# A spectral filter's channel products split by parity of the frequency, with 64-row tails in both row halves, and the skip weights added on GpSimd

## The chip, the cores and the metric

The kernel runs on one core of one Trainium2 chip. The metric is the device time of one execution in microseconds (us); smaller is better. All data are 32-bit floats.

A core has five engines that this text calls as the profile does. PE is TensorE, which multiplies matrices out of SBUF into the banks of PSUM; PEld are its loads of the stationary operand. DVE is VectorE, ACT is ScalarE, POOL is GpSimd, and SP is the engine whose queue issues most DMAs. Each engine works through its own instructions in the order in which the program lists them, and waits for the others by semaphores.

## What is computed

The input x has 2048 rows and 640 channels. The output mixes two branches with a gate for each row: a state-space branch (a long convolution along the rows, its kernel made from 128 modes for each channel, with a skip term) and a branch that filters x in a two-dimensional Fourier domain (rows and channels).

```python
def _A_ref(u, log_A_real, A_imag, C_real, C_imag, log_dt, D_skip):
    ...
    P = jnp.exp((A * dt[:, None])[:, :, None] * pos[None, None, :])
    K = 2.0 * jnp.einsum("dn,dnl->dl", C, P).real
    ...
    Kf = jnp.fft.rfft(K, L2)
    Uf = jnp.fft.rfft(u_t, L2)
    y = jnp.fft.irfft(Uf * Kf[None, :, :], L2)[:, :, :L]
    ...
    return y + u * D_skip[None, None, :]

def _B_ref(x, w_r, w_i):
    X = jnp.fft.rfft2(x, axes=(-2, -1))
    W = w_r + 1j * w_i
    y = jnp.fft.irfft2(X * W, s=(S, D), axes=(-2, -1))
    return y

g = sigmoid((x * gate_w).sum(-1, keepdims=True))
return g * a + (1 - g) * b
```

## The kernel before

Every Fourier transform is a product with a table of sines and cosines on PE. The length of 4096 along the rows is taken apart in two stages (`stage1`, `stage2`); the transform along the 640 channels, which only the filter has, is done by four tables of 160 or 161 columns in the forward direction and by two tables of 321 columns backward.

The program is five phases. Phase P makes the parameters of the convolution kernel. Phase A (its first half, up to line 442) transforms x along the rows and stores the result in device memory (`u_d`). Its second half, the filter (lines 445 to 599), runs 9 turns (eight of 128 rows of frequencies, one of 64). Phase B makes the convolution kernel in 40 steps of 16 channels (`mags`, `phases`, `trig`, `prods`, `kgen`; five steps share one group, since ACT changes its table between exponentials and sines). Phase C transforms the first quarter of that kernel along its length. Phase D multiplies the transforms, goes back and mixes with the gate; it begins when all the others have been issued.

The order of the work is written out by hand. Phases A and C form one stream of the program and phases P and B another; both are generators that yield a cost after each piece of PE work. `merge((194.0, ga), (76.8, gl))` in line 229 always continues the stream with the smaller sum of yielded costs divided by its weight. The two streams are first advanced without a cost up to a fixed point in phase A (`T.pin`, in the second of its four quarters). So the yields and the two weights decide which pieces stand beside which on each engine.

One turn of the filter has these parts, taken in an order that overlaps three turns. `front` (line 471) loads a turn's rows and its weights `ww`, and folds the 640 channels into sums and differences `fg`: DVE takes one half of them and GpSimd the other (lines 487, 488). `transposes` (line 492) brings `fg` to channels on partitions in three chunks, `CH`, of 128, 128 and 65 rows, and later `pm` back in three chunks, `CF`, of 107 rows. `channels` (line 511) makes four products, each in a bank of its own: for each of two parities one matmul over 128 rows and one over the 65 rows of the last chunk. ACT copies two of the four banks to `bc`; DVE adds and subtracts them with the other two (lines 526, 527). `filt` (line 529) multiplies by the weights on DVE. `back1` (line 545) goes back along the channels for 128 rows at a time (17 blocks in all): two products of three matmuls with 107 rows and 321 columns, one copied by ACT to `o`, and two DVE instructions that add or subtract the two halves into `qq`, the second with a reversed output. `back2` (line 560) makes the last product with `qq` and stores it. The three PSUM banks of pool `f_ps` serve all of these.

In phase B, `kgen` (line 685) makes the convolution kernel for 8 columns of channels in one bank. After every second step four small matmuls with the identity (line 703) add the skip weights `dsk` to the column of position 0; ACT then copies the bank to `kt` (line 704). After every tenth step SP stores `kt` to `k_d` (line 706); there is one buffer for `kt`. The store shares SP's queue with the filter's loads.

## Time and profile before

| | us |
|---|---|
| three runs | 604.54, 610.11, 607.86 |
| median of the runs | 607.86 |
| profiled execution, from its first to its last instruction (span) | 605.9 |
| L696, PE, phase B's products, busy | 63.0 |
| L639 and L650, PE, phase B's exponents and phases, busy | 58.9 and 43.3 |
| L681 and L683, GpSimd, phase B's products, busy | 55.4 and 55.5 |
| L703, PE, skip weights, busy (160 instructions) | 5.4 |
| mean granted clock of PE | 0.963 |

For the profiled execution the span is the time on record; it lies 1.96 us under the median of the runs and inside their spread.

In the profile a line like "L552 PE MATMUL p_eo<-td,pmt 107*128 107x321 f32 x204 | 67.5, 450 | ..." reads: line 552 of the kernel, engine, operation, the tile written and the tiles read, rows by columns of the stationary operand, rows by columns of the moving one, how many; then the time in which at least one of them ran, in us; the mean duration of one, in ns; and the idle time of the engine just before, with what ended it. Each 32-bit matmul of the program is two passes in the profile, so 102 matmuls show as 204. Instructions of one engine overlap a little at their ends, and those of PE a good deal, so count times mean is more than the busy time. A row of busy tenths divides the span into 40 slices of 15.1 us, one digit each; 9 is 90% or more.

### The profile page before, as it was taken

What the parts mean: (1) busy time and instruction counts of PE and PEld (TensorE: products, weight loads), DVE (VectorE), ACT (ScalarE), POOL (GpSimd) and SP (SyncE); (2) the same over time, 40 slices, a digit from 0 to 9 for tenths busy, and PEclk for the clock granted to TensorE, in tenths of its full rate; (3) what the DMA queues carried; (4) which work ended last, traced back from release to release, by engine and by line L of the source; (5) the groups of instructions that cost most, each with busy time, mean ns of one, the idle gap of its engine ahead of it and who ended that gap; (6) DMA issues with size and microseconds to landing.
All of it is one profiled execution on the core that took longest, in us unless ns stands there. A gap on an engine that the chain in (4) does not pass through costs nothing. (4 is left out here: it accounts for less than half of the span.)

```text
span 605.9 us, 16674 instructions
## 1 busy us (share of the span) xinstructions
PE 537.6 (89%) x7084; PEld 409.0 (68%) x7084; DVE 496.4 (82%) x748; ACT 364.5 (60%) x659; POOL 263.0 (43%) x246
## 2 busy tenths in 40 slices
PE   9598979988989989989889989898969999999875
PEld 7586647766766667666667676656859877787651
DVE  5971597598899998999998899879397696995965
ACT  4556775476857777899697897798712322232120
POOL 4931153054346344444515344416253447547533
PEclk9999999999979997999897999999998999999979
DMA  8777203235612321243250232006684989879767
GB/s 342 292 283 264 90 2 130 92 133 196 245 45 66 100 85 41 79 125 125 67 140 22 55 96 110 29 23 212 212 346 146 364 274 287 313 254 322 241 211 269
DMA packets 48082, 101.96 MB, mean 168 GB/s; under 512 B 3316, under 2 KB 32776, under 8 KB 46248
## 3 DMA queue, kind: packets, MB, share of 16 engines
q1 hardware_dynamic: 24888, 67.74, 32.1%
q10 hardware_dynamic: 20080, 22.52, 11.9%
q0 software_dynamic: 3040, 10.65, 5.3%
q8 instruction: 55, 0.90, 0.6%
q14 instruction: 19, 0.16, 0.1%
HBM read 60.91 MB, written 39.98 MB: 167 GB/s over the span
## 5 line engine op out<-in xcount | busy, mean ns | idle before, releaser
L349 PE MATMUL p_s<-t,w 128*64 128x160 f32 x1056 | 91.6, 311 | 11.2 <-ACT ut L383 6.0
L681 POOL TENSOR_TENSOR y<-e,sc 128x512 f32<-128x512 f32 x40 | 55.4, 1384 | 89.2 <-DVE x L676 46.7
L349 PEld LDWEIGHTS p_s<-t,w 128*64 128x64 f32 x1056 | 75.9, 137 | 22.3 <-ACT ut L383 6.6
L641 ACT ACTIVATE e<-p_e 128x512 f32<-128x512 f32 x120 | 68.6, 602 | 23.6 <-PE p_e L639 21.4
L683 POOL TENSOR_TENSOR y<-e,sc 128x512 f32<-128x512 f32 x40 | 55.5, 1388 | 44.9 <-ACT sc L667 32.0
L696 PE MATMUL p_k<-x,y 128*32 128x64 f32 x2560 | 63.0, 227 | 11.2 <-POOL y L681 6.1
L696 PEld LDWEIGHTS p_k<-x,y 128*32 128x32 f32 x2560 | 45.2, 112 | 39.6 <-issue 24.2
L552 PE MATMUL p_eo<-td,pmt 107*128 107x321 f32 x204 | 67.5, 450 | 3.9 <-ACT pmt L506 3.9
L337 ACT COPY t<-p_s 128x512 f32<-128x512 f32 x40 | 24.5, 621 | 69.0 <-PE p_s L336 45.5
L653 DVE SCALAR_TENSOR_TENSOR q<-q,p_p 128x512 f32<-128x512 f32 x80 | 53.4, 680 | 13.5 <-ACT q L652 13.3
L639 PE MATMUL p_e<-rm,par 128*128 128x512 f32 x120 | 58.9, 520 | 5.2 <-ACT e L641 3.7
L803 POOL TENSOR_TENSOR t<-ma 64x320 f32<-64x320 f32 x32 | 27.9, 873 | 64.2 <-DVE ma L798 54.8
L652 ACT ACTIVATE q<-p_p 128x512 f32<-128x512 f32 x80 | 46.4, 591 | 6.6 <-PE p_p L650 6.2
L552 PEld LDWEIGHTS p_eo<-td,pmt 107*128 107x128 f32 x204 | 37.7, 194 | 18.4 <-ACT pmt L506 6.4
L678 DVE TENSOR_TENSOR x<-e,cx 128x1024 f32<-128x1024 f32 x40 | 48.5, 1212 | 1.9 <-ACT cx L669 1.9
L817 PE MATMUL p_i<-t,w 128*64 128x160 f32 x528 | 45.1, 308 | 4.4 <-POOL t L804 3.4
L336 PE MATMUL p_s<-c,kt 128*64 128x128 f32 x640 | 44.3, 277 | 3.9 <-DVE mb L799 2.0
L336 PEld LDWEIGHTS p_s<-c,kt 128*64 128x64 f32 x640 | 39.5, 138 | 12.2 <-issue 6.9
L650 PE MATMUL p_p<-rp,par 128*128 128x512 f32 x80 | 43.3, 546 | 4.6 <-DVE q L653 4.5
L819 ACT COPY s<-p_i 128x640 f32<-128x640 f32 x32 | 21.8, 693 | 38.8 <-PE p_i L817 38.7
L817 PEld LDWEIGHTS p_i<-t,w 128*64 128x64 f32 x528 | 39.1, 141 | 8.9 <-POOL t L804 4.0
L798 DVE TENSOR_TENSOR ma<-p_s,us 128x640 f32<-128x640 f32 (+1 forms) x36 | 28.2, 784 | 20.3 <-PE p_s L349 13.3
(153 smaller groups left out, 1186.4 us busy)
## 6 DMA issues: line engine op xcount, KB each, us to landing
u_d<-ut SPq DMA_DIRECT2D x32, 320.0 KB, 3.2
us<-u_d ACTq DMA_DIRECT2D x16, 640.0 KB, 6.0
s_d<-s ACTq DMA_DIRECT2D x15, 640.0 KB, 6.7
t<-s_d SPq DMA_DIRECT2D x14, 640.0 KB, 5.7
ww<-in_w_l SPq DMA_DIRECT2D x8, 642.0 KB, 3.8
ue<-u_d SPq DMA_DIRECT2D x8, 640.0 KB, 4.1
k_d<-kt SPq DMA_DIRECT2D x4, 1280.0 KB, 8.7
kt<-k_d SPq DMA_DIRECT2D x8, 640.0 KB, 5.9
```

Of the source, the lines that this page charges most:

```text
L336: nc.tensor.matmul(p[64 * ri:64 * ri + 64, j, :], src(i + j), e1[ri], start=True, stop=True)
L349: ins = nc.tensor.matmul(p[64 * j:64 * j + 64, i, 160 * ri:160 * ri + 160], w2[:, x, 64 * ri:64 * ri + 64], t1[:, x // 2 if x < 32 else K0 ...
L552: P.matmul(p[:, :E], st.pmt[:DC, c, w, j, :], tv[:DC, w, c, :], start=c == 0, stop=c == 2)
L639: P.matmul(p[:, :], pars[t], rm[:, c:c + 512], start=True, stop=True)
L641: st.exp = S.activation(ef[:, c:c + 512], p[:, :], AF.Exp)
L652: S.activation(qf[:, c:c + 512], p[:, :], AF.Copy, bias=MAGIC)
L653: V.scalar_tensor_tensor(out=qf[:, c:c + 512], in0=qf[:, c:c + 512], scalar=MAGIC, in1=p[:, :], op0=ALU.subtract, op1=ALU.subtract)
L678: V.tensor_tensor(out=x[:, 0].rearrange("p d (h j) -> p d h j", h=2), in0=e[:, :, 0:64].rearrange("p d (h j) -> p d h j", h=2), in1=cx.uns ...
L681: ins = G.tensor_tensor(out=y[:, 1], in0=e[:, :, 64:96], in1=sc[:, 0], op=ALU.mult)
L683: G.tensor_tensor(out=y[:, 0], in0=e[:, :, 64:96], in1=sc[:, 1], op=ALU.mult)
L696: P.matmul(st.pb[32 * r:32 * r + 32, o, :], y[:, ri, 4 * qq + JR[r], :], x[:, ri, 4 * qq + JR[r], :], start=t % 2 + qq + 1 - ri == 0, stop ...
L817: T.mm = P.matmul(p[x:x + 64, i // 2, 160 * (i % 2):160 * (i % 2) + 160], T.w3[:, k0 + h + i, x:x + 64], t2[:, h + i, :], start=True, stop ...
```

## The change

The channels are stored in another order (`PERM`, applied on the host to the inputs and undone on the output), so that the folds of `front` read both halves forward. The last chunk of both transposes is now rows 97 to 225 of the 321, a full 128 rows: its lower 64 rows hold the tail of one parity and its upper 64 rows that of the other (rows that a tail doesn't need meet zeros in the table). `CF` and the two tables of 321 columns go; the backward products use tables of 161 columns, of the same build as the forward ones.

A new generator, `product`, serves both directions. It takes two banks at once, one for each parity (`part`), and two right-hand tables (`i`). It issues four matmuls of 128 rows and 160 or 161 columns, then four of 64 rows, alternating between the lower and the upper row half. It yields 0.27 after each of the first four and 0.54 at the end. Before, the forward half yielded 0.54 for each pair of matmuls and the backward half 0.57 for each of its matmuls.

In `channels` two calls of `product` take the place of the four banks. ACT's two copies and DVE's four instructions keep their number and size, but each now takes both tables of one parity. In `back1` one call takes the place of the two products. Then for each of the two banks ACT makes a signed copy of 161 columns to `o` and DVE a sum and a difference of 161 columns into a new tile `z`. Last, GpSimd subtracts and DVE adds 320 columns of `z` each into `qq`.

In `kgen` the four matmuls with the skip weights go. After every tenth step GpSimd adds all of a quarter's skip weights to `kt` before the store. The yield of `kgen` stays 0.88, and the weights of the merge stay as they are.

```diff
-CH = ((0, 128), (193, 321), (128, 193))
-CF = ((0, 107), (107, 214), (214, 321))
+CH = ((0, 128), (193, 321), (97, 225))
+PERM = np.concatenate([np.arange(160), 319 - np.arange(160), 320 + np.arange(160), 639 - np.arange(160)])
...
+    ev0, co, se, so = np.cos(ev), np.cos(od), np.sin(ev), np.sin(od)
     se[:, [0, 160]] = 0
...
+    co[160] = 0
+    so[0] = 0
+
+    def blocks(a, b):
+        n, m = a.shape[1], b.shape[1]
+        t = np.zeros((128, n + m + 161))
+        t[:, :n], t[:, n:n + m] = a[:128], b[32:160]
+        t[31:64, n + m:2 * n + m] = a[128:]
+        t[64:96, n + m:n + 2 * m] = b[:32]
+        return t
...
+    td = np.concatenate([blocks(ev0, co), blocks(so, se), blocks(ev0, co.T), blocks(se, so.T), *(ce[a:b, None] for a, b in CH)], 1)
...
+    u, log_a, a_i, c_r, c_i, log_dt, d_skip, gate_w = (v[..., PERM] if v.ndim == 3 else v[PERM] for v in (u, log_a, a_i, c_r, c_i, log_dt, d_skip, gate_w))
...
-        fwd = (((tabs[0], 0), (tabs[1], 1)), ((tabs[2], 1), (tabs[3], 0)))
+        for n, m in ((161, 160), (160, 161), (161, 161), (161, 161)):
+            tail = td[:, o + n + m:o + n + m + 161]
+            tabs.append(((td[:, o:o + n], tail[0:64, :n]), (td[:, o + n:o + n + m], tail[64:128, :m])))
+            o += n + m + 161
+        fwd, bwd = tabs[:2], tabs[2:]
+        sc = td[:, o:o + 3]
...
-        tv = td[:, 0:6 * E].rearrange("p (w c e) -> p w c e", w=2, c=3)
+
+        def product(banks, lhs, tab):
+
+            for part, p in enumerate(banks):
+                for i in (0, 1):
+                    n = tab(i)[part][0].shape[1]
+                    P.matmul(p[:, 161 * i:161 * i + n], lhs(i, part), tab(i)[part][0], start=i == 0, stop=False)
+                    yield 0.27
+            for i in (0, 1):
+                for part, p in enumerate(banks):
+                    n = tab(i)[part][0].shape[1]
+                    P.matmul(p[:, 161 * i:161 * i + n], lhs(i, 2, part), tab(i)[part][1], start=False, stop=i == 1)
+            yield 0.54
...
-                (G if t else V).tensor_tensor(out=fg[:nl, t, :, 1:160], in0=fo[:nl, t, :, 1:160], in1=fo[:nl, t, :, 319:160:-1], op=ALU.add)
-                (G if t else V).tensor_tensor(out=fg[:nl, t, :, 162:321], in0=fo[:nl, 1 - t, :, 1:160], in1=fo[:nl, 1 - t, :, 319:160:-1], op=ALU.subtract)
-            G.tensor_copy(fg[:nl, :, :, 0:161:160], fo[:nl, :, :, 0:161:160])
+                (G if t else V).tensor_tensor(out=fg[:nl, t, :, 1:160], in0=fo[:nl, t, :, 1:160], in1=fo[:nl, t, :, 160:319], op=ALU.add)
...
-                    S.activation(dst[:n, c, :, 0:nl // 64], v, AF.Copy, scale=td[:n, 6 * E + c:6 * E + c + 1])
+                    S.activation(dst[:n, c, :, 0:nl // 64], v, AF.Copy, scale=sc[:n, c:c + 1])
...
-            for dst, x, w in ((0, 3, 1), (1, 2, 1), (2, 0, 0), (3, 1, 0)):
-                p = bank("p_d")
-                for par, (tab, c) in enumerate(fwd[w]):
-                    v = p[:nl, 161 * par:161 + 160 * par]
-                    P.matmul(v, st.ft[:, c, x, :nl], tab[0], start=True, stop=False)
-                    P.matmul(v, st.ft[:65, 2, x, :nl], tab[1], start=False, stop=True)
-                    yield 0.54
-                i = dst % 2
-                if dst < 2:
-                    S.copy(bc[:nl, i], p[:nl, :E])
-                else:
-                    V.tensor_tensor(out=xx[:nl, 0, i], in0=p[:nl, :E], in1=bc[:nl, i], op=ALU.add)
-                    V.tensor_tensor(out=xx[:nl, 1, i], in0=p[:nl, :E], in1=bc[:nl, i], op=ALU.subtract)
+            for w in (1, 0):
+                xs = (3, 2) if w else (0, 1)
+                pp = [bank("p_d") for _ in xs]
+                yield from product([p[:nl] for p in pp], lambda i, c, h=None: st.ft[slice(64 * h, 64 * h + 64) if c == 2 else slice(128), c, xs[i], :nl], lambda i: fwd[w])
+                for part, p in enumerate(pp):
+                    e = slice(0, 161) if part == w else slice(161, 321)
+                    n = 161 - (part != w)
+                    pv = p[:nl, 0:322].rearrange("p (i e) -> p i e", i=2)[:, :, 0:n]
+                    if w:
+                        S.copy(bc[:nl, :, e], pv)
+                    else:
+                        V.tensor_tensor(out=xx[:nl, 0, :, e], in0=pv, in1=bc[:nl, :, e], op=ALU.add)
+                        V.tensor_tensor(out=xx[:nl, 1, :, e], in0=pv, in1=bc[:nl, :, e], op=ALU.subtract)
...
-            o = wk.tile([128, E], F32, tag="o", name="o")
+            o = wk.tile([128, 2, 161], F32, tag="o", name="o")
+            z = wk.tile([128, 646], F32, tag="z", name="z")
             qq = st.qq[j] = wk.tile([128, D], F32, tag="qq", name="qq")
-            for w in (1, 0):
-                p = bank("p_eo")
-                for c in range(3):
-                    P.matmul(p[:, :E], st.pmt[:DC, c, w, j, :], tv[:DC, w, c, :], start=c == 0, stop=c == 2)
-                    yield 0.57
-                if w:
-                    S.copy(o[:, :], p[:, :E])
-                else:
-                    V.scalar_tensor_tensor(out=qq[:, 0:321], in0=o[:, :], scalar=T.sg[0], in1=p[:, :E], op0=ALU.mult, op1=ALU.add)
-                    V.scalar_tensor_tensor(out=qq[:, 639:320:-1], in0=o[:, 1:320], scalar=T.sg[1], in1=p[:, 1:320], op0=ALU.mult, op1=ALU.add)
+            pp = [bank("p_eo") for _ in (1, 0)]
+            yield from product([p[:, :] for p in pp], lambda i, c, h=None: st.pmt[slice(64 * h, 64 * h + 64) if c == 2 else slice(128), c, 1 - i, j, :], lambda i: bwd[1 - i])
+            for part, p in enumerate(pp):
+                S.activation(o[:, part], p[:, 0:161], AF.Copy, scale=T.sg[0])
+                for v in (0, 1):
+                    c = 322 * v + 161 * part
+                    V.tensor_tensor(out=z[:, c:c + 161], in0=p[:, 161:322], in1=o[:, part], op=(ALU.add, ALU.subtract)[v])
+            zv = z.rearrange("p (v k) -> p v k", v=2)
+            qv = qq.rearrange("p (c d) -> p c d", c=4)
+            G.tensor_tensor(out=qv[:, 2:0:-1], in0=zv[:, :, 0:160], in1=zv[:, :, 161:321], op=ALU.subtract)
+            V.tensor_tensor(out=qv[:, 0:4:3], in0=zv[:, :, 0:160], in1=zv[:, :, 161:321], op=ALU.add)
...
-                yield from transposes(prv.pm, prv.pmt, prv.nl, CF, True)
+                yield from transposes(prv.pm, prv.pmt, prv.nl, CH, True)
...
-                             start=t % 2 + qq + 1 - ri == 0, stop=False)
+                             start=t % 2 + qq + 1 - ri == 0, stop=t % 2 + qq - ri == 4)
...
-            for r in range(4):
-                P.matmul(st.pb[32 * r:32 * r + 32, :, 31], T.id[:, 32 * r:32 * r + 32], dsk[:, c, i:i + 8], start=False, stop=True)
             S.copy(kt[:, i:i + 8, :], st.pb[:, :, :])
             if t % 10 == 9:
+                G.tensor_tensor(out=kt[:, :, 31], in0=kt[:, :, 31], in1=dsk[:, c, :], op=ALU.add)
                 nc.sync.dma_start(T.k_d[c], kt[:, :, :])
```

24 lines of the change are left out of this document (4 added, 20 removed).

## The prediction

> **What bounds the kernel now.** I read the page first, then the busy time by windows, then first and last starts of a few lines, then the groups by line and shape, last the timeline around one turn of the filter.
>
> ```profile
> PE 537.6 (89%) x7084; PEld 409.0 (68%) x7084; DVE 496.4 (82%) x748; ACT 364.5 (60%) x659; POOL 263.0 (43%) x246
> DVE  5971597598899998999998899879397696995965
> ```
>
> Over the whole span PE is the busiest. But the second row (VectorE in 40 slices of 15 us) has a stretch of 8s and 9s from slice 11 to 28, and that is where the change lies. So I ask for that stretch alone.
>
> ```profile
> L482 DVE TENSOR_TENSOR fo<-ue x9: 809/814/826, 153.4 to 343.6; 128x640 f32<-128x640 f32 x8, 64x640 f32<-64x640 f32 x1
> L566 PE MATMUL p_i<-qq,w x68: 430/432/741, 200.9 to 421.9; 128*128 128x320 f32 x68
> L704 ACT COPY kt<-p_k x20: 575/592/647, 86.9 to 436.1; 128x512 f32<-128x512 f32 x20
> L663 DVE TENSOR_SCALAR aq<-q x40: 677/686/2447, 72.5 to 424.6; 128x1024 int32<-128x1024 int32 x40
> ...
> core 0: us, PE busy (x) PEld busy (x) DVE busy (x) ACT busy (x) POOL busy (x), PEclk, DMA share, GB/s
> 155.00:421.00 266.00, 243.14 (x2854) 177.09 (x2853) 244.90 (x367) 213.79 (x399) 114.39 (x100) 0.95 0.29 89
> 421.00:437.00 16.00, 13.97 (x316) 12.21 (x312) 6.80 (x10) 13.11 (x25) 5.62 (x5) 1.00 0.62 212
> 160.00:320.00 160.00, 143.81 (x1594) 106.53 (x1594) 153.01 (x230) 125.25 (x230) 71.54 (x61) 0.93 0.31 97
> ```
>
> Columns of the windows: length, then busy us of each engine. The filter (first L482 to last L566) runs from about 155 to 421; beside it run the 40 steps of the SSM kernel's stage (one L663 each, the last at 424.6, its last copy at 436.1). In the filter's stretch DVE is busy 244.9 of 266 (92%) and 153.0 of 160 (95.6%) in its first 160 us; PE shows 243.1, as much. The tie is broken by what the two wait for:
>
> ```profile
> DVE q L653 <- ACT q L652: 10.8, 10, 2.9
> ```
>
> That is the largest wait of DVE there, half of its idle time, and DVE's busy time is work end to end, while PE's contains the latency of matmuls whose successor waits (a modelled 0.43 us for a pass that follows its neighbour after 0.29, below). I take DVE as the bound of the filter's stretch.
>
> **The order between the two streams.** The merge keeps its weights, 194.0 and 76.8, and the second is the sum of the yields of the 40 steps: 40 x (0.60 + 0.44 + 0.88) = 76.8, so 1.92 a step. The first, before: rest of phase A after the pin 44.75; filter 9 x (1.35 + 4.32) + 17 x 1.08 + 9 x 1.35 + 17 x 3.42 = 139.68; first piece of phase C 9.6; together 194.03. Both streams end together. After: a forward turn yields 2 x (4 x 0.27 + 0.54) = 3.24 in place of 4.32 and a back block 1.62 in place of 3.42: the filter is 139.68 - 9 x 1.08 - 17 x 1.80 = 99.36 and the stream 153.71. One unit still draws 76.8 / 194 = 0.396 units of the other, so beside the filter go 99.36 x 0.396 / 1.92 = 20.5 steps instead of 28.8, and when the first stream is out, 76.8 - 60.85 = 15.95 units, 8.3 steps, are left with nothing beside them. This is the largest effect that I see. Nothing in the diff corrects it.
>
> **Cost 1, DVE in the filter's stretch.**
>
> ```profile
> L653 DVE SCALAR_TENSOR_TENSOR q<-q,p_p 128x512 f32<-128x512 f32 x80 | 53.4, 680 | 13.5 <-ACT q L652 13.3
> L678 DVE TENSOR_TENSOR x<-e,cx 128x1024 f32<-128x1024 f32 x40 | 48.5, 1212 | 1.9 <-ACT cx L669 1.9
> L663 DVE TENSOR_SCALAR aq<-q 128x1024 int32<-128x1024 int32 x40 | 30.4, 759 | 0.3
> L677 DVE TENSOR_TENSOR x<-e,sx 128x512 f32<-128x512 f32 x40 | 27.1, 678 | 0.0
> L676 DVE SCALAR_TENSOR_TENSOR x<-e,sx 128x512 f32<-128x512 f32 x40 | 27.1, 678 | 0.6 <-ACT sx L668 0.6
> ...
> L557 DVE SCALAR_TENSOR_TENSOR qq<-o,c,p_eo 128x321 f32<-128x321 f32 x17 | 9.2, 543 | 2.7 <-PE p_eo L552 2.7
> L558 DVE SCALAR_TENSOR_TENSOR qq<-o,c,p_eo 128x319 f32<-128x319 f32 x17 | 9.1, 538 | 0.0
> L526 DVE TENSOR_TENSOR xx<-p_d,bc 128x321 f32<-128x321 f32 x16 | 7.7, 482 | 2.0 <-PE p_d L520 2.0
> L879 DVE TENSOR_TENSOR oe<-p_e,gate 128x480 f32<-128x480 f32 x16 | 10.5, 657 | 0.5
> L879 DVE TENSOR_TENSOR oe<-p_e,gate 128x320 f32<-128x320 f32 x8 | 3.9, 482 | 1.3 <-PE p_e L161 1.3
> L487 DVE TENSOR_TENSOR fg<-fo 128x318 f32<-128x318 f32 x8 | 6.9, 857 | 0.0
> L487 POOL TENSOR_TENSOR fg<-fo 128x318 f32<-128x318 f32 x8 | 10.9, 1363 | 15.0 <-PE p_t L503 12.6 <-DVE fo L483 2.4
> ...
> 418.22 1.28 DVE L653 SCALAR_TENSOR_TENSOR q<-q,p_p 128x512 f32<-128x512 f32 x2
> ```
>
> Two L653 in a row end after 1.28, not 2 x 0.68: an instruction that follows another costs 0.08 less than its row. A step is 2 x 680 + 759 + 678 + 678 + 1212 = 4,687, less 6 x 80: 4.21 us. The 8.3 steps that leave take 34.9 us of DVE with them. A back block loses L557 and L558 (543 + 538 - 160 = 921 ns). It gains four additions of 161 columns from a PSUM bank: L879 falls by 175 ns from 480 to 320 columns, so 307 at 160, 227 in a row, 908 for four. It gains one addition of 320 columns with both inputs in SBUF, for which L487 is the nearest row: 857, or 777 in a row. So 1,685 - 921 = 764 ns a block, 13.0 us for 17. Ends: 5.7 if that last one runs as fast as a PSUM one of its width (482 less 80, as L526), 23 if it, or a neighbour behind it, waits out the GpSimd subtraction issued just ahead of it (1,363). I keep 13.0, because L487 stands beside just such a GpSimd partner.
>
> The Trainium skill (SBUF — State Buffer, Who interferes with whom) says that a VectorE instruction with two SBUF inputs and a GpSimd instruction that reads SBUF shut each other out for a whole instruction. The rows agree: L487 857 against 482 of L526 at the same width. By that rule alone the new pair collides in all 17 blocks and the sum stands at the 23 end.
>
> The rest of the forward half keeps its four DVE additions and two copies, split by parity; reversed reads become forward ones; I cost both at nothing, between -0.1 and +0.1 us each. The filter's DVE work is then 244.9 - 34.9 + 13.0 = 223.0. PE and ACT get lighter beside it, so I take the share of the denser window, 95.6%: 233 us instead of 266. The filter ends at 155 + 233 = 388. (At 92%: 397; with no idle time at all: 378.)
>
> **Cost 2, what runs alone.** Phase C's first piece with the 2 steps beside it: about 10 of the 16 us from 421 to 437, the other 6 being the last three products and the copy, which still close the stage. Then 8.3 steps alone.
>
> ```profile
> L641 ACT ACTIVATE e<-p_e 128x512 f32<-128x512 f32 x120 | 68.6, 602 | 23.6 <-PE p_e L639 21.4
> L652 ACT ACTIVATE q<-p_p 128x512 f32<-128x512 f32 x80 | 46.4, 591 | 6.6 <-PE p_p L650 6.2
> L667 ACT ACTIVATE sc<-aq,c 128x512 f32<-128x512 f32 x40 | 28.8, 719 | 8.1 <-DVE aq L663 7.8
> L669 ACT ACTIVATE cx<-aq,c 128x512 f32<-128x512 f32 x40 | 27.3, 683 | 1.2 <-DVE x L678 1.2
> L666 ACT ACTIVATE sc<-q 128x512 f32<-128x512 f32 x40 | 25.4, 635 | 13.5 <-DVE q L653 13.5
> L668 ACT ACTIVATE sx<-q 128x512 f32<-128x512 f32 x40 | 24.1, 602 | 6.4 <-DVE x L677 4.2 <-DVE q L653 1.9
> L641 ACT ACT_TABLE_LOAD x8 | 10.3, 1283 | 2.7 <-PE p_e L639 2.6
> L668 ACT ACT_TABLE_LOAD x8 | 10.3, 1283 | 0.1
> ...
> 419.88 0.69 DVE L663 TENSOR_SCALAR aq<-q 128x1024 int32<-128x1024 int32 x1
> 424.63 0.69 DVE L663 TENSOR_SCALAR aq<-q 128x1024 int32<-128x1024 int32 x1
> ```
>
> ACT needs 3 x 602 + 2 x 591 + 719 + 683 + 635 + 602 + 0.5 x 592 + 20.6 / 40 = 6.4 us a step, about 5.8 with overlap between neighbours; DVE needs 4.2. Inside a group of five a step takes 4.75 (last two rows), without its exponentials. I take 6.1 for a step: 8.3 x 6.1 = 50.6. Ends: 4.75 if the exponentials hide, 7.1 if they and the sines of each group of five run strictly in turn (4.75 + 15 x 0.6 / 5 + 2.6 / 5).
>
> **Sum.** 388 + 10 + 50.6 + 6 = 454.6 where the last copy and its store now close the stage at 437: 17.6 later. Phase D behind it is not touched. Span 605.9 + 17.6 = 623.5; the median of the runs, 607.86, lies 2.0 over the span: **625.5 us**.
>
> **The other edits.**
>
> ```profile
> L552 PE MATMUL p_eo<-td,pmt 107*128 107x321 f32 x204 | 67.5, 450 | 3.9 <-ACT pmt L506 3.9
> 248.28 2.43 PE L552 MATMUL p_eo<-td,pmt 107*128 107x321 f32 x8
> 247.70 0.49 PEld L696 LDWEIGHTS p_k<-x,y 128*32 128x32 f32 x30 [0.44 <-issue]
> 250.64 0.25 PE L703 MATMUL p_k<-dsk,c 128*32 128x8 f32 x8
> ```
>
> PE: a pass of 321 columns costs (2.43 - 0.43) / 7 = 0.286, so a back block falls from 12 x 0.286 = 3.4 to 8 x 0.143 + 8 tail passes at half of that if the two row halves run side by side, 1.7; with none side by side 2.3. 17 blocks: 19 to 29 us. Forward tails: 144 passes x 0.143, half saved, 10, or 0. Skip products: 20 x 0.25 = 5. So 24 to 44 us off PE. None of it shortens a stretch that DVE fills, and in the last 8.3 steps ACT covers PE; so zero in the sum. The Trainium skill (TensorEngine Tiling (Array Packing), Key Properties) says that a change of tiling mode drains TensorE, and the 0.44 before L696 agrees; 35 products with two changes each would give back up to 31 us of the 44. Where PE bounds, that sentence takes most of the gain.
>
> Each product now takes two of three banks at once and frees them only behind ACT and DVE, so the next one's second half can wait. No row shows it: 0 to about 1 us for each of 35 products. I take 0, since PE has the room, and keep 20 for the range. ACT: two copies of 161 for one of 321, under 0.4 us x 17, covered in the filter. GpSimd: 17 subtractions and four additions at up to 1.4 us, beside 114 busy of 266. The four additions stand behind its queued products, and the store of the SSM kernel, on SP's queue, stands behind them, and behind that the loads of the next turn: four times, a few us, loads with a turn's lead; between 0 and 4 us, I take 0. The smaller table (half the bytes) loads before its use either way.
>
> **The rivals.**
> Faster: PE's queue in order, not DVE, paced all this (for it: PE busy 243 of 266; against: 95.6% on DVE). With PE light, DVE runs without gaps (223.0) and a lone step goes at 4.75: 155 + 223 + 10 + 39.4 + 6 = 433, 4 earlier; with the 5.7 end, 426: 597 us. It decides only if a lone step goes below some 5.0 us.
> No change: DVE full, extra 5.7, ACT's 5.8: 155 + 216 + 10 + 48 + 6 = 435 to 443: 606 to 614. For it: the added adds have no row. Against: DVE was never without idle time.
> Much slower: banks or the port make the filter longer: +20 on top: 645 us.
>
> **How the numbers follow.** Forecast (slower, 614 to 637) 0.50; much slower 0.15; no change 0.20; faster 0.15. The range takes the forecast, the no-change case and most of both outer ones: 598 to 648. A difference under 1% (6 us; the three runs lie from 604.5 to 610.1) cannot be told from none: faster 0.15, same 0.20, slower 0.65.
>
> **What would show it.** Right: the filter's last product near 388, DVE above 90% up to there, then some 50 us in which the first stream shows nothing, ACT above 85% and PE under 60%, and phase D's length unchanged at 169. Wrong: a filter ending after 400 (PE waiting for banks, or DVE rows of the new additions above 0.4 us), or before 375 (PE was the bound), or lone steps spaced under 5 us.

## The result, and the profile after

The kernel after takes 653.61 us (median of four runs, 648.77 to 655.72), the kernel before beside it 606.20 (603.41 to 610.11): a ratio of 1.0764, with a 95% interval of 1.0696 to 1.0831. That is 47.4 us slower. The direction was forecast, the size was not: 625.5 was predicted, and the range ended at 648.

Three lines of the page after: the sums of the engines, then VectorE's busy tenths and PE's granted clock in 40 slices, now of 16.3 us.

```profile
PE 557.5 (85%) x6992; PEld 410.4 (63%) x6992; DVE 509.9 (78%) x799; ACT 371.6 (57%) x676; POOL 277.7 (42%) x267
...
DVE  6952687797998998899999991470769799696975
...
PEclk9889979999898797898999975775559999999999
```

The plateau of 8s and 9s that ran to slice 28 before ends at slice 24 now. Behind it stand six slices with a DVE of 0 to 7 and a clock of 5 to 7, which the kernel before does not have. The first of them, from 392 to 409 us, still belongs to the filter. The busy time by windows puts numbers to it. The windows are the filter (first fold on DVE to last product on PE), the stretch from there to DVE's first instruction of phase D, and phase D. After:

```profile
core 0: us, PE busy (x) PEld busy (x) DVE busy (x) ACT busy (x) POOL busy (x), PEclk, DMA share, GB/s
154.20:411.60 257.40, 226.16 (x2287) 157.55 (x2287) 225.65 (x376) 181.60 (x348) 107.56 (x103) 0.87 0.26 82
411.60:489.30 77.70, 55.50 (x853) 37.98 (x853) 40.57 (x57) 54.11 (x94) 27.91 (x23) 0.60 0.29 111
489.30:653.70 164.40, 141.56 (x1712) 111.44 (x1708) 134.69 (x199) 40.97 (x66) 83.03 (x89) 1.00 0.81 270
```

And before, by the same milestones:

```profile
153.40:421.90 268.50, 245.64 (x2883) 178.55 (x2882) 247.34 (x374) 216.00 (x403) 115.53 (x101) 0.95 0.29 91
421.90:437.70 15.80, 13.77 (x319) 12.26 (x319) 5.91 (x9) 12.21 (x23) 5.18 (x5) 1.00 0.63 214
437.70:605.90 168.20, 145.48 (x1712) 115.36 (x1708) 134.24 (x199) 41.08 (x66) 83.08 (x89) 0.97 0.82 276
```

The filter begins 0.8 later, is 11.1 shorter, the stretch behind it is 61.9 longer, phase D 3.8 shorter: 47.8 in all, which is the difference of the spans (653.7 and 605.9). The filter lost 11.1 us although 8 of its 29 steps left it. And DVE, which was busy 92.1% of it, is busy 87.6% of it now.

The mean hides where the idle time stands. The filter taken apart at 392.2 us, and the wait that ends its hole:

```profile
154.20:392.20 238.00, 208.53 (x2178) 146.91 (x2177) 219.38 (x365) 169.74 (x327) 106.43 (x102) 0.90 0.28 88
392.20:408.60 16.40, 15.94 (x98) 9.59 (x102) 3.27 (x6) 9.15 (x19) 0.38 (x1) 0.54 0.07 21
...
404.47 0.69 DVE L664 SCALAR_TENSOR_TENSOR q<-q,p_p 128x512 f32<-128x512 f32 x1 [10.09 <-ACT q L663]
```

For 238 us DVE is 92.2% busy. Then it has 3.3 us of work in 16.4 us: the last turn, of 64 rows, is alone in the filter, and its transposes and its back block stand on PE and ACT among the 15 exponentials of a group of phase B. In the kernel before, DVE was busy 17.4 of the filter's last 20 us.

The new instructions of a back block, from the groups by line and shape (busy us, mean ns; then the idle time ahead of them and its cause):

```profile
L565 DVE TENSOR_TENSOR z<-p_eo,o 128x161 f32<-128x161 f32 x68 | 17.9, 315 | 6.3 <-ACT o L562 6.2
L569 DVE TENSOR_TENSOR qq<-z 128x320 f32<-128x320 f32 x17 | 14.9, 876 | 0.0
L568 POOL TENSOR_TENSOR qq<-z 128x320 f32<-128x320 f32 x17 | 17.9, 1053 | 45.5 <-DVE z L565 41.1 <-PE p_t L512 2.8 <-PE p_p L661 1.6
L562 ACT ACTIVATE o<-p_eo,c 128x161 f32<-128x161 f32 x34 | 12.4, 393 | 15.9 <-PE p_eo L471 14.4 <-ACT o L562 0.8 <-ACT e L652 0.6
```

DVE has 17.9 + 14.9 = 32.8 us there, where lines 557 and 558 had 18.3: 14.5 more, and 13.0 were predicted. The last two rows show long waits: GpSimd's subtraction stood 41.1 us for DVE, ACT's copy 14.4 for PE. DVE's own waits in the filter (us in total, times, longest):

```profile
DVE q L664 <- ACT q L663: 18.2, 8, 10.1
DVE z L565 <- ACT o L562: 6.2, 4, 3.0
```

In the lonely stretch the timeline has one integer pass over the phases (`aq`) for each step:

```profile
416.69 0.69 DVE L674 TENSOR_SCALAR aq<-q 128x1024 int32<-128x1024 int32 x1
430.02 0.69 DVE L674 TENSOR_SCALAR aq<-q 128x1024 int32<-128x1024 int32 x1
435.17 0.69 DVE L674 TENSOR_SCALAR aq<-q 128x1024 int32<-128x1024 int32 x1
439.56 0.69 DVE L674 TENSOR_SCALAR aq<-q 128x1024 int32<-128x1024 int32 x1
459.38 0.69 DVE L674 TENSOR_SCALAR aq<-q 128x1024 int32<-128x1024 int32 x1
465.28 0.69 DVE L674 TENSOR_SCALAR aq<-q 128x1024 int32<-128x1024 int32 x1
473.03 0.69 DVE L674 TENSOR_SCALAR aq<-q 128x1024 int32<-128x1024 int32 x1
```

Inside a group of five a step follows after 4.4 to 7.8 us, where before it was 4.75; the 13.3 us from 416.69 to 430.02 hold the first piece of phase C, which keeps PE for 11.0 us (L332, from 416.66). Between the groups (439.56 to 459.38) 19.8 us pass, in which the next group's exponentials and phases are made and DVE has nothing: the two runs of ACT's table stand strictly one behind the other.

### The profile page after: what moved, and what is told of

Same layout as the page of the kernel before. It is cut to its first block, busy times and chain, and to the rows that moved or that the text cites. A ratio compares the mean times of both kernels' runs of the same rounds, so it can differ in the third digit from the quotient of the medians.

```text
span 653.7 us, 16616 instructions
## 1 busy us (share of the span) xinstructions
PE 557.5 (85%) x6992; PEld 410.4 (63%) x6992; DVE 509.9 (78%) x799; ACT 371.6 (57%) x676; POOL 277.7 (42%) x267
## 4 chain that ended last, share of the span: by engine, by line
PE 46%; DVE 27%; ACT 10%; issue 6%; DMA 6%; POOL 3%; SPq 0%; ACTq 0%; DVEq 0%; POOLq 0%
PE p_s L332 7%; PE p_s L345 7%; PE p_e L650 6%; PE p_k L707 5%; PE p_i L577 3%; PE p_i L827 3%; PE p_t L512 3%; DVE t L814 3%; PE p_p L661 2%; DVE ma L808 2%; DVE q L664 2%; PE p_eo L466 2%; DVE mb L809 2%; DMA u_d<-ut 2%; DVE x L689 2%
## 5 line engine op out<-in xcount | busy, mean ns | idle before, releaser
L707 PE MATMUL p_k<-x,y 128*32 128x64 f32 x2560 | 79.2, 250 | 30.1 <-POOL y L692 12.5
L345 PE MATMUL p_s<-t,w 128*64 128x160 f32 x1056 | 93.3, 316 | 10.4 <-ACT ut L379 5.6
L707 PEld LDWEIGHTS p_k<-x,y 128*32 128x32 f32 x2560 | 54.5, 125 | 71.2 <-issue 30.4
L650 PE MATMUL p_e<-rm,par 128*128 128x512 f32 x120 | 63.8, 570 | 7.6 <-ACT e L652 6.2
L689 DVE TENSOR_TENSOR x<-e,cx 128x1024 f32<-128x1024 f32 x40 | 48.7, 1217 | 18.0 <-ACT cx L680 17.9
L661 PE MATMUL p_p<-rp,par 128*128 128x512 f32 x80 | 45.2, 574 | 8.8 <-DVE q L664 8.6
L332 PEld LDWEIGHTS p_s<-c,kt 128*64 128x64 f32 x640 | 39.9, 143 | 10.5 <-issue 7.4
L827 PE MATMUL p_i<-t,w 128*64 128x160 f32 x528 | 42.5, 300 | 4.4 <-POOL t L814 3.4
L332 PE MATMUL p_s<-c,kt 128*64 128x128 f32 x640 | 43.9, 282 | 2.3 <-DVE mb L809 2.0
L332 PE MATMUL p_s<-c,u 128*64 128x128 f32 x640 | 42.8, 283 | 2.6 <-ACT ut L379 2.5
L827 PEld LDWEIGHTS p_i<-t,w 128*64 128x64 f32 x528 | 36.6, 137 | 9.2 <-POOL t L814 4.0
L332 PEld LDWEIGHTS p_s<-c,u 128*64 128x64 f32 x640 | 36.7, 140 | 8.7 <-issue 4.4
L650 PEld LDWEIGHTS p_e<-rm,par 128*128 128x128 f32 x120 | 24.9, 216 | 26.5 <-ACT e L652 16.9
```

What stands on the lines that cost most here:

```text
L332: nc.tensor.matmul(p[64 * ri:64 * ri + 64, j, :], src(i + j), e1[ri], start=True, stop=True)
L345: ins = nc.tensor.matmul(p[64 * j:64 * j + 64, i, 160 * ri:160 * ri + 160], w2[:, x, 64 * ri:64 * ri + 64], t1[:, x // 2 if x < 32 else K0 ...
L650: P.matmul(p[:, :], pars[t], rm[:, c:c + 512], start=True, stop=True)
L661: P.matmul(p[:, :], pars[t], rp[:, c:c + 512], start=True, stop=True)
L689: V.tensor_tensor(out=x[:, 0].rearrange("p d (h j) -> p d h j", h=2), in0=e[:, :, 0:64].rearrange("p d (h j) -> p d h j", h=2), in1=cx.uns ...
L707: P.matmul(st.pb[32 * r:32 * r + 32, o, :], y[:, ri, 4 * qq + JR[r], :], x[:, ri, 4 * qq + JR[r], :], start=t % 2 + qq + 1 - ri == 0, stop ...
```

## The experiments

All ratios are to the kernel before in the same set of runs, with 95% intervals. Two things were to be told apart: what the unbalanced merge costs, and what the new products cost. The second left several suspects.

**The merge alone, and the products alone.** e1 takes the kernel before and unbalances the merge as the change does; e2 takes the kernel after and balances it (its first stream's yields sum to 153.71).

```diff
 e1, in the kernel before
-            merge((194.0, ga), (76.8, gl))
+            merge((244.9, ga), (76.8, gl))
 e2, in the kernel after
-            merge((194.0, ga), (76.8, gl))
+            merge((153.7, ga), (76.8, gl))
```

> The kernel before, with only the first weight of the merge changed from 194.0 to 244.9, so that its own filter gets ahead and 8.3 steps of phase B are left alone, as in the changed kernel. No product is changed. Theory 1 (the order of the two streams is what costs): the filter ends near 393 instead of 422, then some 70 us with the lone steps, span 630 to 645, the granted clock in the lone stretch near 0.6. Theory 2 (the banks that a product holds cost most, the order little): the lone steps make up for the earlier end, 600 to 615.

> The changed kernel with the first weight set to the sum of its own yields, 153.7, so that both streams end together again. Theory 1: the lone stretch goes, no window below a clock of 0.8 around it, 610 to 622 (DVE has some 13 to 15 us more to do between 155 and phase D, at 88 to 92% busy). Theory 2: the filter's own waits stay and grow with more steps beside it, 630 to 645.

e1: 628.27 us, 1.0397 (1.0324 to 1.0470). e2: 627.71 us, 1.0386 (1.0307 to 1.0465). e1 comes out a little below the range of its first theory, e2 between its two. So each half costs about 24 us, and 1.0397 x 1.0386 = 1.080 is the 1.076 measured for both within its interval: the two add. Windows of e1 (filter, stretch behind it):

```profile
140.00:383.20 243.20, 224.95 (x2461) 164.82 (x2462) 214.69 (x330) 186.06 (x348) 102.15 (x90) 0.97 0.29 92
383.20:458.70 75.50, 54.54 (x896) 37.17 (x896) 43.37 (x61) 56.91 (x98) 27.37 (x21) 0.67 0.27 106
```

With the old products, DVE's share of a thinned filter is 214.69 / 243.20 = 88.3%, and the stretch behind it 75.5 us, almost as after. Both belong to the merge and not to the products. The idle time stands at the filter's end here too:

```profile
140.00:363.20 223.20, 205.41 (x2204) 151.88 (x2205) 203.70 (x313) 170.40 (x317) 98.06 (x86) 0.97 0.30 93
363.20:383.20 20.00, 19.55 (x259) 12.95 (x258) 10.99 (x18) 15.66 (x31) 4.09 (x4) 1.00 0.27 78
```

That is 91.3% up to there, and 11.0 of the last 20 us. Windows of e2 (filter, stretch behind it, phase D):

```profile
157.60:437.30 279.70, 239.25 (x2785) 168.30 (x2781) 258.10 (x424) 216.24 (x412) 128.48 (x119) 0.92 0.26 83
437.30:456.80 19.50, 15.60 (x375) 13.44 (x375) 9.59 (x13) 14.78 (x27) 7.39 (x8) 1.00 0.79 291
456.80:625.60 168.80, 144.09 (x1712) 113.27 (x1708) 134.87 (x199) 41.06 (x66) 82.94 (x89) 0.98 0.81 272
```

The lonely stretch is gone. The filter begins 4.2 later than before, takes 11.2 longer, with DVE busy 92.3% of it as before (92.1%), and 3.7 more pass behind it. From here on the question is these 24 us.

**One bank at a time.** e3 (weight 194.0) and e4 (153.7) make a product for one parity at a time, so that it holds one bank of the three.

```diff
...
-            pp = [bank("p_eo") for _ in (1, 0)]
-            yield from product([p[:, :] for p in pp], ...
-            for part, p in enumerate(pp):
+            for part in (0, 1):
+                p = bank("p_eo")
+                yield from product(p[:, :], part, ...
```

> The changed kernel, but product makes one parity at a time: one bank is taken, filled by its two full and two 64-row matmuls and evicted before the next is taken. The row halves of the two parities no longer alternate; yields and weights sum as in the changed kernel. Theory 1: the banks are not what holds the filter up; it ends between 405 and 415 as before, 648 to 658. Theory 2: the filter ends near 390, DVE above 93% busy in it, 628 to 638.

> Both: one parity at a time, and the first weight 153.7. Theory 1: like the changed kernel with that weight, within 4 us. Theory 2: 10 to 20 us below it. If each holds in part, near 600 to 610, which would be no slower than the kernel before.

e3: 651.47 us, 1.0759 (1.0671 to 1.0848), as after. e4: 646.38 us, 1.0671 (1.0594 to 1.0748), 19 us above e2, which neither theory had. Its filter:

```profile
158.60:458.00 299.40, 266.53 (x2787) 185.11 (x2785) 260.32 (x425) 218.50 (x412) 126.00 (x120) 0.90 0.24 78
```

With one bank at a time PE is busy 27 us more than in e2 (16 of them in its 64-row passes: 57.6 against 41.2) and the filter is 20 longer. That speaks against the prediction's view that PE has room to spare. It does not clear the banks, since the wait for them stays. The kernel after has it in the second block of a turn, for example here:

```profile
237.53 0.71 PE L466 MATMUL p_eo<-td,pmt 128*128 128x161 f32 x4
238.40 0.81 PE L471 MATMUL p_eo<-td,pmt 64*128 64x161 f32 x4
242.87 1.01 DVE L565 TENSOR_TENSOR z<-p_eo,o 128x161 f32<-128x161 f32 x4
244.17 1.44 PE L466 MATMUL p_eo<-td,pmt 128*128 128x161 f32 x4
245.54 1.44 PE L471 MATMUL p_eo<-td,pmt 64*128 64x161 f32 x4
```

The first parity with its tails is done at 239.2. The second begins at 244.2, when DVE's additions have freed the first block's banks. In the kernel before, a copy of ACT alone freed one of a block's two banks; now every bank waits for ACT's copy and for DVE. The longest pause between two neighbouring passes of a block is 2.2 us before, 6.6 after, 7.2 in e2 and 7.6 in e4. PE does work of the other stream in the pause, so it is no loss by itself; no run took it away, and its price stays open.

**Moving the last two instructions between DVE and GpSimd.** e5 gives the last addition to GpSimd, e6 the subtraction to DVE; both with weight 153.7.

```diff
 e5
-            V.tensor_tensor(out=qv[:, 0:4:3], ... op=ALU.add)
+            G.tensor_tensor(out=qv[:, 0:4:3], ... op=ALU.add)
 e6
-            G.tensor_tensor(out=qv[:, 2:0:-1], ... op=ALU.subtract)
+            V.tensor_tensor(out=qv[:, 2:0:-1], ... op=ALU.subtract)
```

> The changed kernel with weight 153.7, and the last addition of each back block (320 columns, two SBUF inputs) moved from DVE to GpSimd beside the subtraction. DVE loses about 17 x 0.8 = 14 us between 155 and phase D, GpSimd gains 18. If DVE's work sets the filter's length (92% busy in it, as in the kernel before): 612 to 618. If the products' order on PE sets it: 625 to 630, and DVE's busy share falls under 89%.

> The changed kernel with weight 153.7, and the subtraction of each back block moved from GpSimd to DVE. DVE gets 17 more instructions of some 0.4 us in a row (7 us), but no GpSimd partner beside its addition any more (the addition back at 0.48 from 0.88, 7 us less). If DVE's work sets the length and collisions with the partner make half of what it gained: 625 to 631, no change. If the collisions are elsewhere: 632 to 638. If the products' order on PE sets it: 625 to 630 and DVE over 93% busy.

e5: 621.84 us, 1.0300 (1.0233 to 1.0367), between its two forecasts. e6: 634.11 us, 1.0483 (1.0390 to 1.0575). Both intervals overlap that of e2. e5's filter:

```profile
157.90:435.60 277.70, 239.66 (x2785) 171.55 (x2784) 255.04 (x408) 216.49 (x412) 140.80 (x136) 0.92 0.27 84
```

DVE lost the 16.0 us that line 569 has in e2's filter, and its busy time fell by 3.1. Where the rest went, one group of DVE shows, in e2 and then in e5:

```profile
L547 DVE TENSOR_TENSOR mm<-xx,ww 128x642 f32<-128x642 f32 (+1 forms) x9 | 9.7, 1083 | 0.0
```

```profile
L547 DVE TENSOR_TENSOR mm<-xx,ww 128x642 f32<-128x642 f32 (+1 forms) x9 | 11.9, 1324 | 0.0
```

The same multiplication of two SBUF tiles grew from 1083 to 1324 ns as GpSimd got more to do. The Trainium skill (SBUF — State Buffer, Who interferes with whom) says that a DVE instruction with two SBUF inputs contends with a GpSimd instruction that reads SBUF; the rows agree. DVE's fourteen groups of this kind in the fold and the filter's weights (lines 491 to 497 and 542 to 552) grew from 101.4 to 109.8 us together: half of what leaves DVE for GpSimd comes back inside DVE's other rows.

**The skip weights alone, and the forward products alone.** e7 is the kernel before with the skip weights on GpSimd. e12 is the kernel before with the new forward products, the old backward ones, and weight 184.3 (its yields' sum).

```diff
 e7, in the kernel before
...
-            for r in range(4):
-                P.matmul(st.pb[32 * r:32 * r + 32, :, 31], ...
...
+                G.tensor_tensor(out=kt[:, :, 31], in0=kt[:, :, 31], in1=dsk[:, c, :], op=ALU.add)
 e12, in the kernel before
-CH = ((0, 128), (193, 321), (128, 193))
+CH = ((0, 128), (193, 321), (97, 225))
...
+            for w in (1, 0):
+                ...
+                yield from product([p[:nl] for p in pp], ...
```

> The kernel before with the skip weights alone moved to GpSimd: 160 passes of PE go (5.4 us busy), four additions on GpSimd come before the four stores. If DVE bounds: within 3 us of before, 600 to 607. If the store behind GpSimd's queue holds up SP's loads or the next copy into kt: 607 to 615.

> The kernel before with the new forward products alone (two banks, 64-row tails; channels in the old order, backward tables, block and skip weights as before) and the first weight at the sum of its yields, 184.3. DVE's work is that of before. If DVE sets the length: 600 to 610, no change. If what costs lies in the two banks and the split tails: 610 to 620. If PE's relief counts: 592 to 600.

e7: 605.60 us, 0.9980 (0.9927 to 1.0032): nothing. e12: 608.69 us, 1.0053 (1.0024 to 1.0082): 3 us. So some 20 of the 24 are left for the backward half.

**DVE's work: more of it, and less.** e9 is the kernel before with lines 557 and 558 issued twice. e10 (weight 153.7) leaves out the differences of line 565.

```diff
 e9, in the kernel before
+                    for _ in range(2):
                         V.scalar_tensor_tensor(out=qq[:, 0:321], ...
                         V.scalar_tensor_tensor(out=qq[:, 639:320:-1], ...
 e10, in the kernel after
-                for v in (0, 1):
+                for v in (0,):
...
```

> The kernel before with the two DVE instructions of each back block issued twice (the same result again): 17 x 2 x 0.46 = 15.6 us of DVE more, no PE work, wait or weight changed. If DVE's work sets the filter's length at 92% busy: 15.6 / 0.92 = 17 us more, 617 to 625. If PE's order sets it: 603 to 611.

> The changed kernel with weight 153.7, leaving out the second of the two DVE instructions on each bank of the back half (the difference); the last two additions read the sums in its place, so the filter's output is not the reference's. 34 instructions of some 0.24 us in a row: 8 us of DVE less, the same on PE and GpSimd. If DVE sets the length: 8 / 0.92, 616 to 622. If PE's order sets it: 625 to 630.

e9: 620.87 us, 1.0243 (1.0156 to 1.0329). e10: 624.90 us, 1.0332 (1.0251 to 1.0412). The filters of e9 and of e10:

```profile
152.90:434.50 281.60, 248.80 (x2806) 173.95 (x2806) 259.93 (x409) 218.18 (x403) 121.31 (x101) 0.96 0.28 89
```

```profile
159.10:435.80 276.70, 242.39 (x2784) 173.94 (x2784) 252.15 (x391) 216.56 (x412) 129.10 (x120) 0.90 0.27 84
```

In the old order 12.6 us more of DVE make the filter 13.1 longer: there DVE is the bound, and added work costs its full length. (The repeats also hold the block's bank longer; e9 doesn't tell the two apart.) In the new order 5.9 us less of DVE make it 3.0 shorter.

**Less work on PE.** e11 (weight 153.7) leaves out all matmuls of 64 rows.

```diff
-            for i in (0, 1):
-                for part, p in enumerate(banks):
-                    n = tab(i)[part][0].shape[1]
-                    P.matmul(p[:, 161 * i:161 * i + n], lhs(i, 2, part), tab(i)[part][1], start=False, stop=i == 1)
...
```

> The changed kernel with weight 153.7, leaving out all 64-row matmuls (the tails of both directions), so the filter's output is not the reference's: 35 bursts of 0.75 us, 26 us of PE less, and 70 changes of its tiling; the same on DVE. If DVE sets the length: 622 to 630. If PE's order or its drains set it: 600 to 615.

e11: 627.01 us, 1.0335 (1.0274 to 1.0397). Its filter:

```profile
159.80:439.30 279.50, 217.04 (x2504) 150.05 (x2504) 256.45 (x426) 216.84 (x412) 127.49 (x120) 0.87 0.27 83
```

PE is busy 22 us less than in e2, and the filter is 0.2 shorter. So in this order relief of PE is worth nothing, and the tails don't carry the 24 us either.

**The clock in the lonely stretch.** e8 is the kernel after with phase and exponent matmuls repeated in the last steps (the repeats give the same numbers again).

```diff
-                P.matmul(p[:, :], pars[t], rm[:, c:c + 512], start=True, stop=True)
+                for _ in range(2 if t > 34 else 1):
+                    P.matmul(p[:, :], pars[t], rm[:, c:c + 512], start=True, stop=True)
...
-            P.matmul(p[:, :], pars[t], rp[:, c:c + 512], start=True, stop=True)
+            for _ in range(4 if t > 31 else 1):
+                P.matmul(p[:, :], pars[t], rp[:, c:c + 512], start=True, stop=True)
```

> The changed kernel (weight 194.0) with useless repeats in the lone stretch: each phase matmul of steps 32 to 39 is issued four times and each exponent matmul of steps 35 to 39 twice, into the same bank (70 us of added passes at 0.4 to 0.8 us would be 25 to 50 us of PE). If the half clock there comes of PE's low load and lengthens the stretch: the granted clock rises to 0.85 or more and the stretch falls from 77 to 65 to 70 us, 642 to 648 in all. If the stretch is one of ACT and DVE in turn and the clock only follows: 652 to 662.

e8: 649.01 us, 1.0740 (1.0660 to 1.0820), between its two forecasts, with the clock of the first. Its stretch:

```profile
408.00:483.00 75.00, 57.73 (x918) 40.88 (x918) 40.43 (x57) 54.64 (x94) 28.25 (x23) 0.89 0.31 116
```

The clock rose from 0.60 to 0.89 and 2.7 of 77.7 us went. But the repeats took back what the clock gave: in the stretch the phase and exponent products were busy 30.3 us against 21.2, the products p_k and p_s 27.4 against 33.9. So e8 does not price the half clock, and its share in the stretch stays open. In the kernel after, ACT waited there 15.3 us for products of PE (p_k 6.1, p_s 4.5, p_e 4.1, p_p 0.6).

**Placement, the last instructions, and GpSimd's queue.** e13 is the kernel after with the old sums of yields at the old weight. e14 and e15 stand on e2.

```diff
 e13
-                    yield 0.27
+                    yield y
...
-            yield 0.54
+            yield 2 * y
...
 e14
+            st.qq[j] = z
...
-            G.tensor_tensor(out=qv[:, 2:0:-1], ... op=ALU.subtract)
-            V.tensor_tensor(out=qv[:, 0:4:3], ... op=ALU.add)
 e15
-            G.tensor_tensor(out=qv[:, 2:0:-1], in0=zv[:, :, 0:160], in1=zv[:, :, 161:321], op=ALU.subtract)
+            gv = zv if T.gz is None else T.gz
+            G.tensor_tensor(out=qv[:, 2:0:-1], in0=gv[:, :, 0:160], in1=gv[:, :, 161:321], op=ALU.subtract)
+            T.gz = zv
```

> The kernel after with the old sums of yields: 0.36 and 0.72 in place of 0.27 and 0.54 in a forward product, 0.57 and 1.14 in a backward one, and the old weight of 194.0. So every piece of the one stream meets nearly the same pieces of the other as in the kernel before. Placement (the 4.2 us before the filter and the 3.7 us behind it in e2 come from more steps beside phases A and C): both go, ratio 1.02 to 1.025, filter begins near 153.4. Work (only the new instructions count): as e2, 1.035 to 1.04, since the missing step or two return to the filter, where each costs DVE 4.2 us.

> The kernel after with weight 153.7 (e2); it leaves out the last step of each back block, GpSimd's subtraction and DVE's addition, and gives the sums and differences in z to the last product as they are. DVE's work of a back block is then that of the kernel before (four times 315 ns against 543 and 538), and GpSimd has no new instruction there. DVE and GpSimd as the cause of e2's excess: ratio 1.00 to 1.015. PE's and ACT's new order as the cause (two banks at once, two copies, waits between them): 1.025 or more, with DVE's busy time in the filter near 242 and its share below 0.90.

> The kernel after with weight 153.7 (e2); GpSimd's subtraction takes the z of the block before instead of the block's own, so it is the same work but finds its input ready and does not hold up the products of the SSM kernel (y) that stand behind it in GpSimd's queue. This changes what is computed. Queue theory (y is late because the subtraction waits for z at the head of the queue): ratio falls by 0.010 or more below e2's 1.0386, and PE waits less for y. Work theory: as e2 within 0.005.

e13: 637.31 us, 1.0500 (1.0464 to 1.0535). e14: 622.14 us, 1.0255 (1.0190 to 1.0321). e15: 626.59 us, 1.0298 (1.0249 to 1.0347). e13 missed both forecasts. Its filter begins at 155.2, near the old place as the placement theory said, but it is longer than in any run so far but e4; then e14's:

```profile
155.20:447.70 292.50, 251.31 (x2830) 174.25 (x2830) 261.34 (x426) 222.01 (x422) 130.02 (x121) 0.89 0.24 77
```

```profile
160.30:433.60 273.30, 239.50 (x2785) 170.76 (x2784) 244.13 (x409) 216.97 (x414) 109.88 (x103) 0.93 0.27 86
```

Against the kernel before, with the merge as it was, DVE has 14.0 us more to do in e13 and idles 10 more (292.50 - 261.34 = 31.2, against 21.2). Its waits there:

```profile
DVE z L565 <- ACT o L562: 11.9, 8, 4.5
DVE q L664 <- ACT q L663: 10.7, 8, 2.3
```

The first has taken the place of the 2.7 that line 557 waited for PE. e14 has DVE's work of a back block back at its old size, and GpSimd's gone, and still costs 15 us: by its own forecast, PE's and ACT's new order carries these. But only 4.8 of them lie in the filter; it begins 6.9 later, where the lower weight of the first stream puts more steps beside phase A. So e14 does not separate the order from the placement. e13, which has the old placement, begins early and pays in the filter. The last two instructions are worth the other 8 or so (its interval and e2's just touch). e15 comes out between its two forecasts, with an interval that overlaps e2's. It did not do what was meant: GpSimd's subtraction waited 19.5 us there (11.0 for PE's p_i, 8.5 for `z`), as in e2 (19.6). So what GpSimd's queue costs stays open.

**Cutting the ring of waits.** e16, e17 and e18 stand on e13. In e16 DVE takes the copy `o` of the block before, in e17 GpSimd the `z` of the block before, in e18 both last instructions go to GpSimd one turn later.

```diff
 e16
...
-                    V.tensor_tensor(out=z[:, c:c + 161], in0=p[:, 161:322], in1=o[:, part], ...
+                    V.tensor_tensor(out=z[:, c:c + 161], in0=p[:, 161:322], in1=(o if T.go is None else T.go)[:, part], ...
+            T.go = o
 e17: the diff of e15
 e18
...
+        def back1b(st, j):
+            ...
+            G.tensor_tensor(out=qv[:, 2:0:-1], in0=zv[:, :, 0:160], in1=zv[:, :, 161:321], op=ALU.subtract)
+            G.tensor_tensor(out=qv[:, 0:4:3], in0=zv[:, :, 0:160], in1=zv[:, :, 161:321], op=ALU.add)
...
+            for j in range(old.nl // 64 if old else 0):
+                back1b(old, j)
```

> e13 (old yields), but DVE's sums and differences take ACT's copy o of the block before, so they wait for PE alone and not for the copy behind it; all instructions stay. This changes what is computed. In e13 DVE idles 11.9 us ahead of z for o, against 2.7 ahead of L557 in the kernel before. Copy theory (the copy now lies between PE's last product and DVE): 8 us or more come back, ratio 1.037 or less. PE theory (p_eo itself is late, as ACT's 17.1 us of waiting for it says): DVE then waits for p_eo instead, ratio within 0.006 of e13's 1.05.

> e13 (old yields), but GpSimd's subtraction takes the z of the block before, as in e15. This changes what is computed. In e13 PE waits 14.1 us for y in front of p_k, and p_eo stands behind it. Queue theory (the subtraction waits for z, y stands behind it on GpSimd, p_k waits for y, p_eo behind p_k, o and z behind p_eo): PE's wait for y falls by half or more, ACT's for p_eo too, ratio 1.040 or less. Otherwise within 0.006 of 1.05.

> e13 (old yields), but both last instructions of a back block go to GpSimd and are issued one turn later, between the next turn's transposes and its channels, when z has long been ready. Nothing else changes. DVE loses its 15.2 us of L569, GpSimd gains as much and waits for nothing there. If DVE's work and GpSimd's queue together carry e13's 30 us: ratio 1.01 to 1.025. If the rest is PE's and ACT's new order: 1.03 or more.

e16: 640.13 us, 1.0499 (1.0437 to 1.0560). e17: 637.79 us, 1.0456 (1.0389 to 1.0523). e18: 638.36 us, 1.0518 (1.0435 to 1.0600). None moves from e13 by more than its interval. The filter of e18:

```profile
152.30:447.70 295.40, 257.34 (x2830) 178.40 (x2830) 257.32 (x411) 221.69 (x423) 141.88 (x138) 0.87 0.24 76
```

Its waits, of GpSimd in the filter, show that it did not do all that was meant, since GpSimd runs ahead and still meets `z` too early:

```profile
POOL qq L571 <- DVE z L565: 41.3, 12, 6.2
```

DVE, with 15.2 us of line 569 taken off it, is 4.0 less busy than in e13, and the filter is 2.9 longer. In e16 ACT's wait for p_eo remained, and DVE's wait for `o` with it (10.4 us), so the copy was not cut out cleanly. In e17 PE's wait for y did not fall (14.1 to 14.4), but GpSimd's subtraction still waited 34.1 us (17.0 for PE's p_i, 11.4 for its p_eo, 5.7 for `z`), in e13 32.1. So none of the three runs cut the wait that it was made to cut, and the ring is neither shown nor ruled out.

The filters of balanced runs side by side, from the windows shown and the same windows of e6, e12 and e15 to e17 (the merge stands as before in e13 and e16 to e18, and close to it in the others):

| kernel | back blocks | filter us | DVE busy, share | PE busy | clock |
|---|---|---|---|---|---|
| before | old | 268.5 | 247.3, 92.1% | 245.6 | 0.95 |
| e12 | old | 272.6 | 242.7, 89.0% | 248.0 | 0.94 |
| e9 | old, DVE more | 281.6 | 259.9, 92.3% | 248.8 | 0.96 |
| e2 | new | 279.7 | 258.1, 92.3% | 239.3 | 0.92 |
| e6 | new, DVE more | 284.0 | 257.6, 90.7% | 245.2 | 0.91 |
| e15 | new, GpSimd with the `z` before | 274.9 | 255.1, 92.8% | 235.7 | 0.93 |
| e14 | new, without the last step | 273.3 | 244.1, 89.3% | 239.5 | 0.93 |
| e13 | new | 292.5 | 261.3, 89.3% | 251.3 | 0.89 |
| e16 | new, DVE with the `o` before | 301.9 | 262.4, 86.9% | 263.5 | 0.84 |
| e17 | new, GpSimd with the `z` before | 293.6 | 256.5, 87.4% | 255.0 | 0.88 |
| e18 | new, last step on GpSimd | 295.4 | 257.3, 87.1% | 257.3 | 0.87 |

## Why the prediction was right and where it was wrong

- **The two streams** (20.5 steps beside the filter, 8.3 alone): right. 21 stand in the filter's window, and e1 and e2 show that this alone costs some 24 us, half of the loss.
- **DVE's extra work** (13.0, ends 5.7 and 23): right. Its rows give 14.5, the PSUM additions 315 ns (307 predicted), the SBUF one 876 (857), a mean of 475 to 1,466. (The lower end comes to 6.6 by its own rows, not 5.7.) Its work in the filter was 225.65 us against 223.0. By the rule of the Trainium skill alone (SBUF — State Buffer, Who interferes with whom) it would have been 23: the lock exists (e5), but it does not catch every pair in full.
- **The filter's length** (233 us): this step failed. It divided the work by a share of 95.6%, from the densest window of before, and took that share to the filter's end. 87.6% was measured, so 257.4 us: 24 of the 30 us by which the span is above the sum. The reason given, that PE and ACT get lighter, did not raise the share: DVE was 92.2% busy for 238 us, which makes some 9 of the 24 (223.0 / 0.922 = 241.9). Some 13 are the hole behind 392.2 us, and the rest is more work. The prediction has no term for a last turn that is alone while a group's exponentials run. e1 has the hole with the old products, so it comes from the merge. Why DVE keeps 92% and not 95.6 was not tried.
- **What runs alone** (66.6 us): too short by 11. That steps would run alone was right; what sets their time was not. Phase C's piece with the two steps beside it took 16.0 us (411.6 to 427.6) where 10 were taken. The lone steps took 57.6 us (427.6 to 485.2), 6.9 each, where 6.1 were taken and 7.1 was the end at which the exponentials and the sines of a group run strictly in turn; the 19.8 us between 439.56 and 459.38 are that turn. ACT was to be above 85% busy and PE under 60%; in these 57.6 us they were busy 42.0 (73%) and 38.5 (67%), at a clock of 0.56. So "ACT covers PE" failed: ACT waits for PE there. How much of that is the clock stays open (e8).
- **PE's relief, worth nothing**: right in the filter, as far as e11 goes, which also takes away the changes between 128 and 64 rows that go with the tails. That PE has room on both sides is another matter: e4 has 27 us more on PE and loses 19.
- **Two banks at once** (0 to 1 us for each of 35, taken 0): the wait is there, in the second block of a turn, up to 6.6 us long, but what it costs is not shown. e3 and e4 keep it and so say nothing against it. Something in the new order, or in its placement, does cost: e14, without DVE's extra work, is still 15 us above the kernel before. The prediction gave PE's and ACT's new order no term of its own; here DVE waits for ACT's copy, and ACT for the end of the product (11.9 and 17.1 us in e13).
- **The skip weights** (0 to 4, taken 0): right, e7.
- **Phase D unchanged**: nearly; it was 3.8 shorter, at a clock of 1.00 in place of 0.97.
- **The rivals.** Faster (PE paces) falls with e11. No change falls with the result. Much slower was near in time, and that is luck as far as the runs go: the lock is a part of DVE's rows, and the price of the banks is not shown.

What is shown of the 47 us: 24 from the merge, 24 from the products when the weight balances the merge (e2), 30 when the old yields do (e13). Of the latter part, DVE's new work alone would account for about 15 (e9), the new order with its placement for about 15 (e14); together they cost less than their sum. Which part of the order does it stays open. It is not the tails (e11), and for the most part not the forward products (e12). The later freeing of the banks and the wait in GpSimd's queue are seen in the traces, and no run took either away. None of the kernels tried beats the kernel before.

## What to carry to other kernels

When a busy share is carried over to the changed kernel, ask where the stretch ends and what is beside it there: the share kept at 92% until the last turn, and the last 19 us held 6 us of work for the engine. An order that is steered by written-out costs has to be balanced again when a piece's cost entries change; here that alone was half of the loss. And where two engines are both busy above 90%, added work can cost its full length (e9) while work taken off returns little (e10, e11, e18): price additions in full, savings low, and new handovers between engines apart.

## What the runs showed of the hardware

PE's granted clock stayed at a half in a window in which PE was hardly idle. After, in the gap between two groups:

```profile
445.00:460.00 15.00, 13.01 (x69) 6.12 (x60) 1.90 (x3) 10.55 (x19) 0.00 (x0) 0.50 0.00 1
```

The Trainium skill (TensorE: Matmul & The Clock Gate, Part 1: The HAM clock gate) says that the gate halves the clock after an idle window and lifts it after some 3.4 us of sustained work. By the profile's busy time this row does not agree with the second half: 13.0 of 15 us busy and a clock of 0.50. But the ends of matmuls are modelled, so how long the array worked in these 13.0 us is not shown. In the filter, the clock was 0.94 to 0.97 in every table row with the old back blocks and in e1, and 0.84 to 0.93 in every row with the new ones. Whether that costs anything or only follows from the waits was not tried.

Row halves do run side by side. In the kernel after's timeline eight passes of 64 rows take no longer than the four that stand together in the next product, whose other four come later:

```profile
236.44 0.82 PE L471 MATMUL p_eo<-td,pmt 64*128 64x161 f32 x8
...
238.40 0.81 PE L471 MATMUL p_eo<-td,pmt 64*128 64x161 f32 x4
```

The Trainium skill (TensorEngine Tiling (Array Packing), Key Properties) says that tiles work independently, and the eight passes in 0.82 us agree. How much of it is used depends on the order: a product whose tails stand in two bursts of four gets nothing of it, and so it is in 7 of the 17 back blocks of the kernel after.
